# Moving weight differences, a weight product and value loads later in a fused DeltaNet and maxout FFN kernel

## Chip, cores and metric

The kernel runs on one core of one Trainium2 chip. The metric is the device time of the whole kernel in microseconds (us). The kernel before the change took 525.54 us (median of three runs, 525.25 to 526.2).

## The reference

Two blocks follow each other. The first is a DeltaNet recurrence over 768 positions, for 4 batches and 8 heads of dimension 48; the second a feed-forward block on the 3072 tokens that come out, with 384 inputs and 768 hidden units, the largest of three products each:

```python
for t in range(S):
    y[:, :, t] = q_t @ state
    v_old = state.T @ k_t                     # k_t is normalized
    state = state + beta_t * outer(k_t, v_t - v_old)
x = y.transpose(0, 2, 1, 3).reshape(B * S, H * D)
h = np.maximum(np.maximum(x @ w1, x @ w2), x @ w3)
out = h @ w_out
```

## The kernel before

**Tiling.** The positions are cut into 12 chunks of 64; a chunk is handled for all batches and heads at once, and two chunks make a group. The group's 512 tokens then go through the feed-forward block. So there are six periods, `ffn(0)` to `ffn(5)`, and the recurrence of group m+1 is worked into the period m in small portions. The text calls `ffn(0)` the first period and `ffn(1)` the second.

**A period.** `ffn(m)` is a generator. Each `yield` ends a step: in `hidden` a step multiplies one 128-wide slice f of one weight matrix with the tokens (three matmuls at L926, each of which the trace shows as two records) and takes the result out of PSUM, by a copy on ACT (L934) or ReLU (L936), or by a maximum on DVE (L940). The steps of the output multiply h with `w_out` (L958), copy on ACT and store on SP (L967). The first period has 31 steps, 0 to 30: 18 on halves of the tokens for slices 0 to 2, nine on all tokens for slices 3 to 5, four outputs. Later periods have 12 hidden and 8 half output steps.

**Less work from the second period on.** The largest of three products is also x w1 + max(0, x (w2 - w1), x (w3 - w1)), and x w1 w_out is x times one 384 x 384 matrix. So in the first period all three matrices are used; then `less_first(f)` takes w1's slice f from those of w2 and w3 (two subtractions on DVE, L883), `turn_first` transposes two slices of w1 (PE L892, ACT L898), and `both_layers(t)` makes a third of the matrix w1 w_out (PE L906, ACT L913) in w1's place. Later periods use two matrices in `hidden` and add the small matrix in their outputs.

**The recurrence.** For each group the code needs the grams of keys and queries (`gram`, PE L438, mask on DVE L422, copy on ACT L455), the inverse of triangular blocks (`solve`), and then per chunk: `join_z` (L709, copies L712 and L714), `join_u` (L723, L683), `turn_t1` (DVE L632, L634), `old_k` and `old_q` (L740, DVE L752), `new` (L768), `step` (L791, DVE L798), `to_y` (L810, DVE L812), `to_x` (L824, ACT L874). `solve` is a generator too; its pieces are pairs of DVE operations, a product (L565) and a subtraction (L569). The last three pieces write the solution to DRAM (`y_d`, L591) and read it back in another order into `ut` (L600), by SP's queue. The grams go to DRAM (`at_d`, L468) and back as `x_bl` (L515), which opens the next `solve`.

**Weights and values.** A weight comes as raw bits (`fetch`, L215, into one of five buffers `w_bits`) and is converted in the first period by `weights`: three operations on ACT (L238 to L240), and one call later a shift on DVE (L250) and an integer add on POOL (L254). `load_v` (L139) loads a chunk's values, into one of three buffers; `prep_values` scales them on POOL (L287).

**What sets the order.** The whole order is written by hand (`manual_schedule`), one queue for each engine, and each engine works in order. The loops at the end of the kernel run through the steps and issue after each step what tables and conditions say: `EARLY_LINKS` and `FIRST` name portions of the recurrence by letter and chunk or unit (z `join_z`, j `join_u`, d `turn_t1`, k, q `old_k`, `old_q`, u `new`, s `step`, y `to_y`, x `to_x`, g `gram`, t and T transposes of keys and queries, P grams of queries, S pieces of `solve`); `CONVERTED` and `FETCHED` say when weights are converted and fetched; `some(solving, n)` issues n pieces. PSUM buffers come in two rings: `ffn` with two buffers, so a hidden step needs the buffer of the step two before it, and `two` with three buffers for the recurrence and the transposes.

Of the kernel before, what the change touches and what calls it, by code (L numbers as in the profile page):

```python
# [23 lines left out]
def kernel(  # L24
# [31 lines left out]
    nc = tc.nc  # L56
# [23 lines left out]
    def ps_ffn(shape, name):  # L80
        return psum.tile(shape, FP32, name=name, tag="ffn", bufs=2)

    def ps_two(name):
        return psum.tile([128, 2, 512], FP32, name=name, tag="two", bufs=3)
# [24 lines left out]
    def rows(bb):  # L109
        return slice(C * bb, C * (bb + 1))  # L110
# [19 lines left out]
    def load_k(n, queues=one_queue):  # L130
        load(k, kpad[place(n)], n, queues)

    def load_q(n, queues=one_queue):
        load(q, qpad[n % NQ], n, queues)

    def load_v(c, queue=nc.sync):
        vts[c] = work.tile([128, 2, H, D], FP32, name="v_t", bufs=3)
        for bb in range(2):
            queue.dma_start(  # L139
                out=vts[c][rows(bb)].rearrange("p g h d -> p (g h) d"),  # L140
                in_=v[2 * bb : 2 * bb + 2, :, c * C : (c + 1) * C, :].rearrange(
                    "b h p d -> p (b h) d"
                ),
            )
# [66 lines left out]
    def fetch(queue=nc.scalar):  # L211
        if fetched[0] < len(pieces):
            _, src, (a, b) = pieces[fetched[0]]
            st = work.tile([128, 2 * 384], U32, name="w_bits", bufs=5)
            queue.dma_start(  # L215
                out=st.rearrange("p (a b) -> p a b", a=a), in_=src
            )
            staged.append(st)
            fetched[0] += 1
# [66 lines left out]
    def scale(c, nrm):  # L286
        nc.gpsimd.tensor_tensor(  # L287
            out=vts[c], in0=vts[c],
            in1=nrm[:, :, :, None].to_broadcast([128, 2, H, D]), op=ALU.mult,
        )  # L290

    def prep_values(c):

        if c in nrms:
            scale(c, nrms.pop(c))
# [214 lines left out]
    def blocks(m):  # L510
        if m == 1:
            xs[m] = in_wo(0)
        else:
            xs[m] = work.tile([128, 2, HB * BL + HB], FP32, name="x_bl", bufs=1)
        nc.sync.dma_start(  # L515
            out=in_rows(xs[m]),
            in_=at_d[m].rearrange("c f b h j i -> (c f b h) j i"),
        )
# [361 lines left out]
    def less_first(f):  # L880
        part = (slice(None), slice(None), slice(f * 128, (f + 1) * 128))
        for i in (1, 2):
            nc.vector.tensor_tensor(  # L883
                out=w_sb[i][part], in0=w_sb[i][part], in1=w_sb[0][part],
                op=ALU.subtract,
            )

    def turn_first(fs):
        p_f = ps_two("p_t")
        for i, f in enumerate(fs):  # L890
            for t in range(KT):
                nc.tensor.transpose(  # L892
                    p_f[:, i, t * 128 : (t + 1) * 128],
                    w_sb[0][:, t, f * 128 : (f + 1) * 128],
                    ident,
                )
        for i, f in enumerate(fs):
            nc.scalar.copy(  # L898
                w_sb[0][:, :, f * 128 : (f + 1) * 128],
                p_f[:, i, 0 : KT * 128].rearrange("p (t x) -> p t x", t=KT),  # L900
            )

    def both_layers(t):
        p_m = ps_ffn([128, DM], "p_m")
        for f in range(FT):
            nc.tensor.matmul(  # L906
                p_m,
                w_sb[0][:, t, f * 128 : (f + 1) * 128],
                wo_sb[:, f],
                start=(f == 0),  # L910
                stop=(f == FT - 1),
            )
        nc.scalar.copy(w_sb[0][:, t, 0:DM], p_m)  # L913
# [58 lines left out]
    def some(gen, n):  # L972
        for _ in range(n):
            if next(gen, gen) is gen:
                break

    conv = weights()
    solving = solve(0)
# [96 lines left out]
    for n in (2, 3):  # L1075
        masked(pts[n], by_par(pts[n]))
    load_q(4)
    load_v(2)
    solving = solve(1)
    some(solving, 1)  # L1080

# [7 lines left out]
    }  # L1089
    EARLY_LINKS = {  # L1090
        9: "k0 q0", 10: "t0", 11: "t1", 12: "g0", 13: "t2", 14: "g1", 15: "t3",
        16: "g2", 17: "g3", 18: "d0 d1 z0 z1", 19: "j0", 20: "j1 u0", 21: "s0",
        23: "k1 y0 q1", 24: "u1 x0", 25: "s1", 26: "y1", 28: "x1",
    }


    FIRST = {
        0: "f1 s0 S1 S1", 1: "z1 d1 S1 k1 S1 S1", 2: "j1 S1 S1 S1",
        3: "S1 q1 S1 S1", 4: "u1 T4", 5: "y1", 6: "s1 T5", 7: "x1 T6",
        8: "T7", 14: "P4", 15: "P5", 21: "P6", 22: "P7",  # L1100
    }


# [11 lines left out]
    def links(m, names):  # L1115
        for name in names.split():
            f, i = name[0], int(name[1])
            if f in RECURS and m < GROUPS:
                RECURS[f](2 * m + i)
            elif f in MADE and m + 1 < GROUPS:  # L1120
                MADE[f](2 * (m + 1) + i)
            elif f in UNIT and m + 1 < GROUPS:
                UNIT[f](4 * (m + 1) + i)
            elif f == "N" and m + 2 < GROUPS:
                load_blocks(4 * (m + 2) + i)

    def queries(names):
        for name in names.split():
            f, n = name[0], int(name[1])
            if f not in OF_KEYS:  # L1130
                links(0, name)
                continue
            OF_KEYS[f](n)
            if f == "T" and n + 3 < 11:
                load_q(n + 3)

    CONVERTED = {*range(6), *range(11, 25)}
    FETCHED = {8: 1, 12: 1, 13: 1, 14: 1, 18: 2, 19: 2, 20: 1, 21: 1}  # L1140
    for i, _ in enumerate(ffn(0)):
        if 0 < i < 7:
            fetch(nc.sync)
        for _ in range(FETCHED.get(i, 0)):
            fetch(nc.gpsimd)
        if i in (18, 25):
            some(conv, 1)
        if i == 20:
            solving = solve(2)
            some(solving, 1)  # L1150
        if i == 21:
            some(solving, 3)
        queries(FIRST.get(i, ""))
        links(1, EARLY_LINKS.get(i, ""))
        if i in CONVERTED and i != 18:
            some(conv, 1)
        if 3 < i < 14:
            some(solving, (2, 1, 2, 2, 3, 3, 3, 3, 2, 2)[i - 4])
        if i in (5, 7):
            prep_values(i // 2)  # L1160
        if i in (1, 7):
            for n in range(2):
                load_k(8 + 2 * (i > 1) + n, (nc.gpsimd, nc.gpsimd))
        if i == 0:
            load_v(3)
        if i in (0, 2):
            load_q(5 + i // 2)
        if i == 11:
            load_q(11, (nc.gpsimd, nc.gpsimd))
        if i in (10, 21):  # L1170
            load_v(4 + i // 21)
        if i == 18:
            blocks(2)
        if i == 23:
            prep_values(4)
        if i > 21:
            some(solving, (3, 2, 3, 2, 2, 5, 5, 5, 4)[i - 22])
        if i in (27, 28, 29):
            load_blocks(i - 15, nc.sync)
        if i in (15, 17, 19, 22, 25, 27):  # L1180
            less_first((15, 17, 19, 22, 25, 27).index(i))
        if 27 <= i < 30:
            turn_first((2 * (i - 27), 2 * (i - 27) + 1))


    RECURS.update(x=y_blocks, w=read_y, X=turn_y, p=prep_values)
# [2 lines left out]
    for m in range(1, GROUPS):  # L1189
        for i, _ in enumerate(ffn(m)):  # L1190
            if i == 0:
                some(solving, 3)
            if m == 1 and i in (2, 5, 8):
                both_layers(i // 3)
            if m + 2 < GROUPS:
                if i == 6:
                    blocks(m + 2)
                if i == 8:
                    solving = solve(m + 2)
            links(m + 1, LINKS.get(i, ""))  # L1200
            if i > 7:
                some(solving, 3 if i > 8 else 1)
# [29 lines left out]
```

## Time and profile before

| | |
|---|---|
| median of the runs | 525.54 us |
| the profiled execution, whole | 524.22 us |
| its span, first to last instruction | 522.5 us, granted PE clock 0.966 |
| PE, DVE, ACT, POOL busy | 495.1, 311.0, 164.4, 190.6 us |
| 40 to 120 us: PE, DVE busy | 71.25, 70.11 of 80 us |
| 120 to 522 us: PE, DVE busy | 397.77, 211.93 of 402 us |
| first step of `ffn(0)`, of `ffn(1)`, of `ffn(2)` begins | 51.0, 166.0, 250.7 us |

The profile is one execution, read by the hardware profiler. In the slices each digit is the busy share of a fortieth of the span (13 us) in tenths. In the windows, each engine has its busy time and number of instructions, then come the granted PE clock, the share of the DMA engines in use and GB/s. In the time-ordered views a line has start, duration, engine, source line, operation, tiles, shape and number of instructions; a bracket gives the idle time of the engine before it and what ended it.

### The profile page before, as it was taken

Reading aid. Unit: us, or ns where it says so; the run is one execution under the profiler, and the core shown is the slowest. Engines: PE = TensorE matmul, PEld = TensorE weight load, DVE = VectorE, ACT = ScalarE, POOL = GpSimd, SP = SyncE. Lnnn points to the kernel's source line nnn. Section 1 sums busy time; section 2 is a strip of 40 time slices with the busy share of each in tenths; the row PEclk is TensorE's granted clock in tenths of the full one; section 3 lists DMA queues with packets and bytes.
Section 4 is the critical chain, followed back from the end, with each engine's and each line's share of the span. In section 5 each row is a group of like instructions: output and inputs, shape, how many; then the busy total and the mean of one; then the engine's idle time right before and its main releaser. Section 6 shows DMA issues by size and latency. Waiting matters only on the chain.

```text
span 522.5 us, 18030 instructions
## 1 busy us (share of the span) xinstructions
PE 495.1 (95%) x7840; PEld 305.9 (59%) x7840; DVE 311.0 (60%) x695; ACT 164.4 (31%) x302; POOL 190.6 (36%) x314
## 2 busy tenths in 40 slices
PE   6667898989999999999999999999999999999996
PEld 6556686855666555665556565655655555554453
DVE  5876999998995441699652988645897221111100
ACT  5557473776513142200143200242101411011000
POOL 7515155684383844951394780502130000000000
PEclk9855899999999999999999999999999999999999
DMA  8974958476035953444585444823343202220011
GB/s 111 214 154 114 162 163 138 133 154 199 3 89 135 188 90 69 135 125 115 111 157 121 111 131 102 171 43 91 81 109 85 43 3 63 61 61 0 0 30 32
DMA packets 108671, 53.47 MB, mean 102 GB/s; under 512 B 91760, under 2 KB 102928, under 8 KB 108592
## 3 DMA queue, kind: packets, MB, share of 16 engines
q1 hardware_dynamic: 97840, 34.44, 32.3%
q0 software_dynamic: 8640, 17.49, 13.5%
q8 instruction: 62, 1.02, 0.9%
q10 hardware_dynamic: 2112, 0.39, 0.5%
q14 instruction: 17, 0.14, 0.1%
HBM read 39.17 MB, written 13.11 MB: 100 GB/s over the span
## 4 chain that ended last, share of the span: by engine, by line
PE 79%; DVE 12%; ACT 2%; DMA 2%; issue 1%; POOL 1%; SPq 1%; DVEq 0%; ACTq 0%; POOLq 0%
PE p_h L926 34%; PE p_o L958 26%; PE p_g L438 3%; DVE tmp L565 3%; PE p_m L906 2%; PE p_u L768 2%; PE p_y L810 2%; DVE wo_sb L569 2%; DMA kmore<-in_k_dram 2%; PE p_k L740 2%; PE p_j L723 2%; PE p_s L791 1%; PE p_q L740 1%; SPq L120 1%; PE p_z L709 1%
## 5 line engine op out<-in xcount | busy, mean ns | idle before, releaser
L926 PE MATMUL p_h<-xt,w_sb 128*128 128x512 f32 (+1 forms) x522 | 218.9, 564 | 2.8 <-DVE h L940 1.3
L926 PEld LDWEIGHTS p_h<-xt,w_sb 128*128 128x128 f32 x522 | 96.1, 193 | 88.2 <-issue 79.5
L958 PE MATMUL p_o<-wo_sb,h 128*128 128x384 f32 x288 | 97.8, 489 | 0.0
L940 DVE TENSOR_TENSOR h<-h,p_h 128x512 f32<-128x512 f32 (+1 forms) x48 | 29.6, 617 | 90.0 <-PE p_h L926 89.9
L958 PEld LDWEIGHTS p_o<-wo_sb,h 128*128 128x128 f32 x288 | 53.7, 190 | 35.7 <-issue 0.5
L565 DVE TENSOR_TENSOR tmp<-x_bl,y_bl 128x31 f32<-128x31 f32 (+20 forms) x139 | 51.7, 372 | 4.1
L964 ACT COPY o_sb<-p_o 128x384 f32<-128x384 f32 x24 | 11.5, 479 | 134.2 <-PE p_o L958 128.1
L569 DVE TENSOR_TENSOR y_bl<-y_bl,tmp 128x31 f32<-128x31 f32 (+20 forms) x139 | 48.5, 349 | 4.8
L936 ACT ACTIVATE h<-p_h 128x512 f32<-128x512 f32 x30 | 17.9, 597 | 87.7 <-PE p_h L926 84.8
L958 PE MATMUL p_o<-w_sb,xt 128*128 128x384 f32 x120 | 42.0, 486 | 0.0
L396 POOL DMA_DIRECT2D turned<-in_q_dram x72 | 39.1, 551 | 3.9 <-POOL turned L391 2.9
L438 PE MATMUL p_g<-kqt 48*64 48x64 f32 (+1 forms) x1216 | 27.5, 239 | 6.8 <-DVE nt_bl L263 3.8
L438 PEld LDWEIGHTS p_g<-kqt 48*64 48x64 f32 x1216 | 24.3, 139 | 14.8 <-ACT kqt L367 8.0
L958 PEld LDWEIGHTS p_o<-w_sb,xt 128*128 128x128 f32 x120 | 22.8, 190 | 15.9
L120 POOL DMA_DIRECT2D kpad<-in_k_dram x32 | 21.8, 689 | 15.8 <-PE p_s L791 14.3
L287 POOL TENSOR_TENSOR v_t<-v_t,nrm 128x768 f32<-128x768 f32 x12 | 18.2, 1518 | 24.9 <-DVE nrm L266 12.1
L254 POOL TENSOR_TENSOR w_sb<-mant,up 128x384 int32<-128x384 int32 x18 | 18.3, 1018 | 24.3 <-DVE mant L250 21.7
L798 DVE TENSOR_TENSOR st<-st,p_s 48x768 f32<-48x768 f32 (+1 forms) x18 | 17.1, 949 | 15.0 <-PE p_s L791 14.8
L422 DVE TENSOR_TENSOR pt<-p_g,mask 128x512 f32<-128x512 f32 x20 | 13.7, 688 | 15.8 <-PE p_g L438 15.8
L139 POOL DMA_DIRECT2D v_t<-in_v_dram x12 | 9.9, 827 | 35.9 <-PE p_u L768 35.9
L391 POOL MEMSET turned<- 128x96 f32 x18 | 3.3, 191 | 44.8 <-DVE kqt L412 44.8
L768 PEld LDWEIGHTS p_u<-v_t,ut 64*64 64x64 f32 x768 | 13.5, 141 | 7.8 <-issue 7.3
(153 smaller groups left out, 624.5 us busy)
## 6 DMA issues: line engine op xcount, KB each, us to landing
w_bits<-in_moe_w_dram SPq DMA_DIRECT2D x14, 384.0 KB
out_dram<-o_sb SPq DMA_DIRECT2D x48, 96.0 KB
turned<-in_q_dram POOLq DMA_DIRECT2D x72, 48.0 KB, 2.9
kpad<-in_k_dram POOLq DMA_DIRECT2D x32, 96.0 KB, 4.9
y_x<-y SPq DMA_DIRECT2D x16, 192.0 KB
qall<-y_x SPq DMA_DIRECT2D x32, 96.0 KB
ut<-y_d SPq DMA_DIRECT2D x40, 64.0 KB
v_t<-in_v_dram SPq DMA_DIRECT2D x12, 192.0 KB
```

Of the source, the lines that this page charges most:

```text
L120: queues[bb].dma_start(out=dst[rows(bb ^ g), :, 0:D], in_=src[2 * bb + g, :, c * C : (c + 1) * C, :].rearrange("h p d -> p h d"),)
L254: nc.gpsimd.tensor_tensor(out=dst.bitcast(I32), in0=mant_v.bitcast(I32), in1=up_v, op=ALU.add)
L287: nc.gpsimd.tensor_tensor(out=vts[c], in0=vts[c], in1=nrm[:, :, :, None].to_broadcast([128, 2, H, D]), op=ALU.mult,)
L396: (queue, nc.gpsimd)[i].dma_start(out=t[p0 : p0 + 32, bb, at : at + NP * 2 * D].rearrange("p (j x) -> p j x", j=NP), in_=(k, q)[i][2 * bb ...
L438: nc.tensor.matmul(p_g[rows(bb ^ (g * i)), par, c0 : c0 + C * (1 + whole)], kq[:, 0], kq if whole else kq[:, i],)
L565: nc.vector.tensor_tensor(out=t_v, in0=row.to_broadcast(t_v.shape), in1=column.to_broadcast(t_v.shape), op=ALU.mult,)
L569: nc.vector.tensor_tensor(out=rest, in0=rest, in1=t_v, op=ALU.subtract)
L768: nc.tensor.matmul(p_v[rows(bb ^ g), g, i], ut[c % NU][rows(bb), g, h], rhs[rows(bb), g, h],)
L926: nc.tensor.matmul(p_h, w_sb[i][:, t, f * 128 : (f + 1) * 128], xt[:, t, lo : lo + w], start=(t == 0), stop=(t == KT - 1),)
L936: nc.scalar.activation(out=h, in_=p_h, func=mybir.ActivationFunctionType.Relu)
L940: nc.vector.tensor_tensor(out=h, in0=h, in1=p_h, op=ALU.max)
L958: nc.tensor.matmul(p_o, stays, moves, start=(n == 0), stop=(n == len(terms) - 1))
```

## The change

Nothing is computed in another way; operations are issued at other steps or from other queues.

- `less_first`: from steps 15, 17, 19, 22, 25, 27 of the first period to its steps 29, 30 and steps 1, 3, 5, 7 of the second.
- `turn_first`: from steps 27 to 29 of the first period to steps 2, 5, 8 of the second; `both_layers`: from steps 2, 5, 8 of the second to 9, 10, 11.
- Pieces of `solve(1)`: 1, 1, 1, 1, 2, 3, 3, 3, 3, 3, 2 in steps 4 to 14 for 2, 1, 2, 2, 3, 3, 3, 3, 2, 2 in steps 4 to 13.
- The joins of the next group and nearly all that follow them in the first period come one step later (z in 19 for 18, and so on), as do the grams P6 and P7.
- A weight is converted in step 10 and none in 18; the six fetches from step 18 on go by SP's queue for POOL's.
- `load_v(2)` from before the first period to step 3, `load_v(3)` from step 0 to 8, `load_v(5)` from 21 to 22; `prep_values(2)` and `(3)` from steps 5 and 7 to 8 and 12; `load_q(5)` and `(6)` from steps 0 and 2 to 1 and 3.

```diff
     load_q(4)
-    load_v(2)
     solving = solve(1)
...
-        16: "g2", 17: "g3", 18: "d0 d1 z0 z1", 19: "j0", 20: "j1 u0", 21: "s0",
-        23: "k1 y0 q1", 24: "u1 x0", 25: "s1", 26: "y1", 28: "x1",
+        16: "g2", 17: "g3", 19: "d0 d1 z0 z1", 20: "j0", 21: "j1 u0", 22: "s0",
+        24: "k1 y0 q1", 25: "u1 x0", 26: "s1", 27: "y1", 29: "x1",
...
-        8: "T7", 14: "P4", 15: "P5", 21: "P6", 22: "P7",
+        8: "T7", 14: "P4", 15: "P5", 22: "P6", 23: "P7",
...
-    CONVERTED = {*range(6), *range(11, 25)}
+    CONVERTED = {*range(6), *range(10, 18), *range(19, 25)}
...
-            fetch(nc.gpsimd)
-        if i in (18, 25):
+            fetch(nc.gpsimd if i < 18 else nc.sync)
+        if i == 25:
             some(conv, 1)
...
-        if i in CONVERTED and i != 18:
+        if i in CONVERTED:
             some(conv, 1)
-        if 3 < i < 14:
-            some(solving, (2, 1, 2, 2, 3, 3, 3, 3, 2, 2)[i - 4])
-        if i in (5, 7):
-            prep_values(i // 2)
+        if 3 < i < 15:
+            some(solving, (1, 1, 1, 1, 2, 3, 3, 3, 3, 3, 2)[i - 4])
+        if i in (8, 12):
+            prep_values(i // 4)
...
-        if i == 0:
-            load_v(3)
-        if i in (0, 2):
+        if i in (1, 3):
             load_q(5 + i // 2)
...
-        if i in (10, 21):
-            load_v(4 + i // 21)
+        if i in (3, 8, 10, 22):
+            load_v((3, 8, 10, 22).index(i) + 2)
...
-        if i in (15, 17, 19, 22, 25, 27):
-            less_first((15, 17, 19, 22, 25, 27).index(i))
-        if 27 <= i < 30:
-            turn_first((2 * (i - 27), 2 * (i - 27) + 1))
+        if i > 28:
+            less_first(i - 29)
...
+            if m == 1 and 8 < i < 12:
+                both_layers(i - 9)
+            if m == 1 and i in (1, 3, 5, 7):
+                less_first((i + 3) // 2)
             if m == 1 and i in (2, 5, 8):
-                both_layers(i // 3)
+                turn_first((2 * (i // 3), 2 * (i // 3) + 1))
```

## The prediction

> **What bounds the kernel now.** I read the page (busy shares, slices), then ten-microsecond windows, then the time-ordered views of PE, and of DVE, POOL and SP around each gap of PE. "Step n" is a pass of the loop over ffn(0), the first period; "step B n" one over ffn(1), the second.
>
> ```profile
> PE   6667898989999999999999999999999999999996
> DVE  5876999998995441699652988645897221111100
> ```
> ```profile
> 70.00:80.00 10.00, 8.83 (x194) 7.34 (x186) 9.73 (x19) 7.27 (x14) 4.48 (x5) 1.00 0.62 165
> 80.00:90.00 10.00, 8.68 (x166) 7.50 (x166) 9.52 (x21) 2.85 (x5) 5.31 (x7) 1.00 0.91 143
> 110.00:120.00 10.00, 8.24 (x206) 4.22 (x204) 8.25 (x12) 7.74 (x15) 9.63 (x14) 1.00 0.74 203
> 160.00:170.00 10.00, 10.00 (x122) 5.98 (x122) 4.00 (x16) 2.42 (x5) 0.75 (x2) 1.00 0.50 121
> ```
>
> PE (first figure after the window's length) is full from 118 us on, and DVE (third) is full before. So time is won only where PE waits before 118 us, and lost where a wait opens later. The gaps that the change can reach are these; the bracket is PE's idle time and what ended it:
>
> ```profile
> 79.83 0.65 PE L361 MATMUL p_t<-ident,qall 128*128 128x128 f32 x4 [1.17 <-DVE st L798]
> 83.54 0.67 PE L926 MATMUL p_h<-xt,w_sb 128*128 128x256 f32 x2 [1.32 <-DVE h L940]
> ...
> 111.97 2.84 PE L926 MATMUL p_h<-xt,w_sb 128*128 128x512 f32 x6
> 116.17 0.24 PE L723 MATMUL p_j<-z,t 32*32 32x32 f32 x2 [1.36 <-ACT z L712]
> 116.78 0.74 PE L723 MATMUL p_j<-z,t 32*32 32x32 f32 x62 [0.36 <-ACT z L714]
> 117.44 1.12 PE L926 MATMUL p_h<-xt,w_sb 128*128 128x512 f32 x2
> ```
>
> The early pair is 1.17 + 1.32 = 2.5 us. The late one: from 111.97 to 117.44 are 5.47 us, and the same work elsewhere takes 2.77 (a step, 126.44 to 129.22 in the chain) + 0.68 (p_j at 120.28): 2.0 us lost. Why DVE is late at the early pair:
>
> ```profile
> 79.70 0.83 DVE L565 TENSOR_TENSOR tmp<-wo_sb 128x255 f32<-128x255 f32 x1
> 80.56 1.58 DVE L569 TENSOR_TENSOR wo_sb<-wo_sb,tmp 128x255 f32<-128x255 f32 x1
> 82.18 0.42 DVE L565 TENSOR_TENSOR tmp<-wo_sb 128x256 f32<-128x256 f32 x1
> ```
> ```profile
> 78.60 3.27 POOL L287 TENSOR_TENSOR v_t<-v_t,nrm 128x768 f32<-128x768 f32 x2
> ```
>
> Two things stand ahead of st and h in DVE's queue: pieces of the substitution (L565, L569), and the time that a POOL operation takes from them (1.58 us beside one, 0.42 alone).
>
> **What the Trainium skill says.** GPSIMD Engine Reference, section 1 Specifications: its SBUF interfaces are shared with VectorE, with contention for DVE instructions of two SBUF inputs. The rows above agree. DMA: Bandwidth & Descriptors, "Issuing engines are not separate DMA queues": another issuing engine saves only issue time; the trace gives 0.55 to 0.76 us per L215 on POOL. TensorE: Matmul & The Clock Gate, "What's actually happening": after an idle window of about 3.4 us PE falls to half clock. Here PEclk is 1.00 from 70 us on and the waits are under 1.4 us, so I count no change of clock.
>
> **The change part by part.**
>
> *Thinning.* Before step 7's end 3 pieces fewer are issued (1+1+1+1 for 2+1+2+2), and both value products (L287) move from steps 5 and 7 to 8 and 12. I laid DVE's new order out by hand with the durations of before. The st of step 6 ends near 79.0 instead of 79.8 and the maximum of step 7 near 80.2 instead of 83.3: PE reaches step 9 at 81.3, not 83.54. Gain 2.2 us. But all pieces must still be done before the joins. Up to the last piece DVE now also has one more maximum (0.33) and two more shifts L250 (0.27 each), each followed by a POOL L254 that costs it about 0.7 (1.11, 0.99 and 1.02 for rows that take 0.2 to 0.4): 2.3 us, so the solution ends near 100.9 instead of 98.75. Steps 9 to 13 with 3 pieces each push the maximum of step 13 to 98.5 or 99.1 (without, with a full collision with L287), where step 15 needs its buffer; it began at 99.55. The mask of the grams of step 14 comes near 101.3 to 102.0 and holds step 15's transposes. Step 18 thus begins between 0.3 us earlier and 0.4 later than 107.66: the early gain is given back. I take 0, bounds -0.4 and +2.0.
>
> *Joins a step later; differences gone from steps 15, 17, 19; POOL's loads on SP.* DVE loses 1.83 + 2.48 + 2.31 = 6.6 us of L883 between 103.8 and 119, POOL four L215 (2.2 us) in the stretch 114 to 117, and no weights piece stands in ACT's queue before z. z follows step 19, whose 2.77 us cover the landing of the solution (y_d issued near 101, in the trace 11 us from that to the last landing: 112; z1 comes at 113.5). The copies of z are then hidden by step 20. The 2.0 us go, and 0.26 of z (1.54 us at 110.43, 1.28 at 184.75). What is late next: in the built order the copy of step 18's h waits for a PE count reached only at z's end, so step 20 waits some 0.2. Net +2.1; bounds +0.5 (solution 1.6 us later) and +2.3. The six weight loads on SP stand behind the ut loads; their pieces were due 2 us later: 0. SP's x_bl stands behind two of them, whose buffers are free by then: 0.
>
> *Loads of values and queries.* load_v(2) and (3) leave SP's queue at 50.5 (3.9 us of issue) and stand at steps 3 and 8. No wait of PE, DVE or ACT between 50 and 76 us names them or what they push back: 0. v(2) is issued near 67 and needed at 81; v(3) is needed at step 24.
>
> *First period's end.* turn_first leaves the four outputs: three groups of 0.66 us, which return in the second period: 0. The differences of slices 0 and 1 stand after the last pieces. Before, DVE was done here, and idle to 169.94:
>
> ```profile
> 164.21 0.21 DVE L569 TENSOR_TENSOR y_bl<-y_bl,tmp 128x31 f32<-128x31 f32 x1
> 169.94 0.95 DVE L752 TENSOR_TENSOR v_t<-v_t,p_k 128x768 f32<-128x768 f32 x1 [5.52 <-PE p_k L740]
> ```
> DVE starts 2.6 us earlier and is spared three differences (3 x 1.02), so slice 0 is ready near 159.5; step B 0 begins near 161.5. 0, and 1 us at most if DVE is 3 us later. The other four pairs (1.02 each) lie in DVE's idle time of 170 to 212.
>
> *Products later.* The three p_m (3.96 each) move from steps B 2, 5, 8 to B 9, 10, 11, with 0.66 of transposes in their places. PE's sum is the same, but what waits for SP or DVE now has less cover:
>
> ```profile
> 152.44 1.17 SPq L967 DMA_DIRECT2D out_dram<-o_sb  x2
> ...
> 170.69 2.19 SPq L591 DMA_DIRECT2D y_d<-y_bl  x2
> 174.19 4.04 SPq L600 DMA_DIRECT2D ut<-y_d  x8
> ```
> SP runs without a gap from the first output (PE 151.73) to y_d; the last ut packet in the trace ends at 181.9: 30.1 us after. PE came to z1 33.6 us after it (185.3). Now: p_y 1.0, outputs and p_x 12.4, steps B 0, 1, 2 with p_k, p_q 9.9, transposes 0.7, grams 2.0, step B 3 2.8, z0 0.65: 29.45. So z1 waits 0.6 us; bounds 0 and 3. At step B 10 PE needs the maximum of B 9, which DVE reaches 7.9 us after p_s (212.6 to 220.5), behind st, y and the opening of solve(3); PE needs 1.0 + 2.7 + 4.0 = 7.7: 0.3 us, bounds 0 and 0.8.
>
> Sum: 0 + 2.1 - 0.6 - 0.3 = 1.2 us less. The profiled execution took 524.22 (span 522.5 and 1.7 around it), 1.3 below the median of 525.54; the difference applied to the median gives 524.3.
>
> **Rivals.**
> B, the early gain stays: collisions with POOL fall beside operations that read PSUM, step 15 isn't held. Then 2.0 us more: 522.3. For it: DVE's L798 took 0.94 beside L287, undisturbed. Against it: DVE has the same work, and no gap from 65 to 98 us.
> C, slower: z in the second period waits for ut. The chain SP output, blocks, y_d, ut has no slack left. Each us that the landing slips costs PE one; without that wait the sum is -1.8, so from a wait of 2.9 us on (landing 32.3 us after the first output) the kernel is slower by over 1.05. At 3.5 us: 527.2. For it: the last three of the eight ut loads took 1.0, 1.1 and 1.5 us beside values and keys, the first five 0.5 to 0.7 each. Against it: half of ut, z0's, is there at 26.1.
> D, the late wait only changes its name: the solution ends 2.2 us later and its at_d writes now stand ahead of ut on SP, so z waits in step 19 for ut what j0 waited for z: 525.5. Against it: a whole step lies between.
>
> **Chances.** A change of 0.2% (1.05 us) is about what a measurement of this kernel can tell from none. Forecast 0.45 (own range 523.3 to 525.3: 0.25 faster, 0.20 same), B 0.25 (faster), D 0.17 (same), C 0.13 (slower). Faster 0.50, same 0.37, slower 0.13. The range runs from 522.0 (B, and the 0.3 that its late wait may add) to 526.6, C's point of decision; beyond lie C's 0.13 and under 0.07 of B.
>
> **What would show it.** Right: no PE gap of over 0.5 us before L361 near 79 and L926 near 81; a gap before step 15 (ended by DVE h) or its transposes; p_j without a gap; a gap of 0.3 to 1 us in p_z of the second period, ended by ut's landing. Wrong: PE at step 18 before 106.5 (B); a PE gap before p_z at 112 (D); over 2.5 us at p_z in the second period (C); a PE gap at step B 0 ended by L883, or PEclk under 1.00 after 76 us, which nothing above counts.

## The result, and the profile after

The changed kernel takes 529.32 us (median of 6 runs, 528.11 to 529.81) against 525.54 (6 runs, 523.49 to 527.11): ratio 1.0068, 95% interval 1.0045 to 1.0092. It is slower by 3.8 us, where 524.3 was forecast. The profiled execution took 529.45, its span is 527.7, 5.2 more than before: the one profiled before lies 1.3 below its median, so the two traces differ by more than the medians.

The page's slices, and the windows (engines in the order PE, PE's weight loads, DVE, ACT, POOL):

```profile
PE   6666999798999999999999999999999999999996
DVE  5877999946978664449662888654887231111100
PEclk9856899998999999999999999999999999999999
```
```profile
70.00:80.00 10.00, 9.13 (x166) 7.52 (x165) 9.76 (x19) 7.42 (x15) 5.39 (x8) 1.00 1.13 210
80.00:90.00 10.00, 10.00 (x176) 8.85 (x175) 9.66 (x19) 4.94 (x9) 3.53 (x4) 1.00 1.11 162
110.00:120.00 10.00, 9.86 (x211) 4.99 (x210) 4.15 (x10) 6.87 (x14) 6.20 (x10) 1.00 0.64 164
120.00:130.00 10.00, 7.71 (x138) 4.08 (x139) 7.10 (x23) 7.14 (x14) 4.98 (x5) 0.83 0.72 228
160.00:170.00 10.00, 9.30 (x32) 5.35 (x31) 9.24 (x28) 1.76 (x3) 3.36 (x7) 1.00 0.66 155
```

The two places where time was to be won are won: PE is busy 1.3 us more from 80 to 90 and 1.6 more from 110 to 120. What pays for it stands in the slice and window of 120 to 130. Before, PE was busy there for 10.00 of 10 us at full clock; now for 7.71, and the clock is 0.83. The same window before:

```profile
120.00:130.00 10.00, 10.00 (x270) 6.14 (x270) 9.16 (x26) 6.44 (x13) 3.28 (x4) 1.00 0.55 168
```

PE's gaps in the changed kernel, in order of time:

```profile
79.17 0.66 PE L361 MATMUL p_t<-ident,qall 128*128 128x128 f32 x4 [0.19 <-DVE st L798]
...
92.74 1.56 PE L926 MATMUL p_h<-xt,w_sb 128*128 128x256 f32 x6 [1.01 <-DVE h L940]
100.68 1.56 PE L926 MATMUL p_h<-xt,w_sb 128*128 128x256 f32 x6 [2.42 <-DVE h L940]
103.59 0.66 PE L361 MATMUL p_t<-ident,kpad 128*128 128x128 f32 x4 [0.73 <-DVE pt L422]
126.81 4.21 PE L926 MATMUL p_h<-xt,w_sb 128*128 128x512 f32 x6 [2.29 <-DVE tmp L565]
```

The starts of like steps, before and after: step 9 at 83.54 and 81.39 (2.15 ahead), step 18 at 107.66 and 109.58 (1.9 behind), step 21 at 122.06 and 119.87 (but now j1 and u0, 1.9 us, are still to come, so the two are nearly level), B 0 at 165.99 and 168.44 (and 1.97 of transposes fewer ahead of it), the first step of the third period at 250.59 and 255.94. After that the two run alike. So the loss is made at steps 13 to 16, from step 22 to B 0, and in the second period. Step 22 is the new place:

```profile
116.44 2.81 PE L926 MATMUL p_h<-xt,w_sb 128*128 128x512 f32 x6
119.19 0.75 PE L723 MATMUL p_j<-z,t 32*32 32x32 f32 x64
119.87 2.84 PE L926 MATMUL p_h<-xt,w_sb 128*128 128x512 f32 x6
122.64 0.75 PE L723 MATMUL p_j<-z,t 32*32 32x32 f32 x64
123.32 1.20 PE L768 MATMUL p_u<-v_t,ut 64*64 64x48 f32 x64
```

The joins (L723) follow without a gap: the late wait is gone. But then PE stands from 124.52 to 126.81, and the step takes 4.21 instead of 2.84: 2.3 + 1.4 = 3.7 us.

**The bracket misleads.** It names an operation that ended nearby in time, L565, which began at 126.61. In the program as built, step 22 waits for two things: the maximum of step 20, which DVE ended at 120.70, and an integer add of weights (L254) that POOL had made before 112. Both were met four microseconds earlier. What was not there shows in the DMA queues. The first answer is for 118.06 to 124.10, the second for 124.10 to 125.20 (packets, MB, share of the 16 engines):

```profile
q1 hardware_dynamic: 587, 1.76, 82.8%
```
```profile
q1 hardware_dynamic: 118, 0.30, 70.3%
q8 instruction: 1, 0.02, 5.8%
```

Queue q8 brings instructions: by the page it has 62 packets and 1.02 MB in the whole run, so 16 KB each, one for every 126 of the 7840 matmuls. The packet that falls here started at 124.11 and landed at 125.13; PE had issued 2368 matmuls then, and issued none until 126.81. I call this theory F: PE ran out of instructions, it starved. The transfers that the packet met come from SP; the last line is x_bl's issue before the change:

```profile
111.94 0.96 SPq L215 DMA_DIRECT2D w_bits<-in_moe_w_out_dram  x2
117.96 0.33 SPq L515 DMA_DIRECT2D x_bl<-at_d  x1
118.39 2.11 SPq L215 DMA_DIRECT2D w_bits<-in_moe_w_out_dram  x4
```
```profile
115.14 0.34 SPq L515 DMA_DIRECT2D x_bl<-at_d  x1
```

SP keeps its order. x_bl waits until 117.96 for at_d to land, and four weight loads stand behind it and leave with it: 2 MB at once, the burst of what follows, and DMA is 0.99 in use from 119.5 to 124.

The rivals to F: S, PE waits after all for the opening of solve(2), which x_bl holds up in ACT's and DVE's queues; G, the loss is the thinning's give-back, that is, the early gain lost again at steps 13 to 16.

### The profile page after: what moved, and what is told of

Read it like the earlier page. It is cut to its first block, busy times and chain, and to the rows that moved or that the text cites. A ratio compares the mean times of both kernels' runs of the same rounds, so it can differ in the third digit from the quotient of the medians.

```text
span 527.7 us, 18038 instructions
## 1 busy us (share of the span) xinstructions
PE 495.3 (94%) x7840; PEld 305.5 (58%) x7840; DVE 309.3 (59%) x695; ACT 164.5 (31%) x302; POOL 187.0 (35%) x308
## 3 DMA queue, kind: packets, MB, share of 16 engines
q8 instruction: 62, 1.02, 0.8%
## 4 chain that ended last, share of the span: by engine, by line
PE 76%; DVE 13%; DMA 4%; ACT 3%; issue 2%; POOL 1%; SPq 0%; ACTq 0%; DVEq 0%
PE p_h L926 33%; PE p_o L958 25%; PE p_g L438 3%; DVE wo_sb L569 2%; PE p_u L768 2%; PE p_k L740 2%; DVE tmp L565 2%; PE p_q L740 2%; PE p_y L810 2%; PE p_s L791 1%; PE p_m L906 1%; DMA qall<-in_q_dram 1%; PE p_j L723 1%; DMA kpad<-in_k_dram 1%; PE p_z L709 1%
## 5 line engine op out<-in xcount | busy, mean ns | idle before, releaser
L964 ACT COPY o_sb<-p_o 128x384 f32<-128x384 f32 x24 | 11.5, 479 | 133.9 <-PE p_o L958 133.9
L565 DVE TENSOR_TENSOR tmp<-x_bl,y_bl 128x31 f32<-128x31 f32 (+20 forms) x139 | 50.3, 362 | 4.1
L254 POOL TENSOR_TENSOR w_sb<-mant,up 128x384 int32<-128x384 int32 x18 | 18.2, 1009 | 30.2 <-DVE mant L250 17.1
L812 DVE TENSOR_TENSOR y<-qs,p_y 128x768 f32<-128x768 f32 x11 | 10.5, 953 | 20.2 <-PE p_y L810 20.1
L752 DVE TENSOR_TENSOR v_t<-v_t,p_k 128x768 f32<-128x768 f32 x11 | 10.5, 951 | 15.9 <-PE p_k L740 15.9
```

What stands on the lines that cost most here:

```text
L254: nc.gpsimd.tensor_tensor(out=dst.bitcast(I32), in0=mant_v.bitcast(I32), in1=up_v, op=ALU.add)
L565: nc.vector.tensor_tensor(out=t_v, in0=row.to_broadcast(t_v.shape), in1=column.to_broadcast(t_v.shape), op=ALU.mult,)
```

## Experiments

Each ratio is to runs of the kernel before on the same chip (median 524.8 to 525.3), with its 95% interval. Runs named a, c and e alter the changed kernel; those named b, m and d alter the kernel before.

### Where the packet border falls

a_shift puts 120 more PE instructions at the very start:

```diff
-    busy(6, ident)
+    busy(4, ident)
+    p_w = ps_ffn([128, TOK], "p_w")[0:32, 0:32]
+    for _ in range(32):
+        nc.tensor.matmul(p_w, ident[0:32, 0:32], ident[0:32, 0:32])
```


> The changed kernel; two 128-wide warm-up products at the very start are replaced by 32 products of 32 x 32 (some 60 PE matmuls and as many weight loads more, 120 instructions, where PE waits for the first keys anyway). Nothing of the work, its order or its loads changes. Theory F: [...]the packet that starved step 22 is asked for about one step earlier, ahead of the burst of loads: the gap there goes or moves, 525.5 to 527. Theory S: same waits, 529.3 within 0.3. Theory G: 529.3.

a_shift2 puts 64 PE matmuls into p_h ahead of step 14's product:

```diff
                 p_h = ps_ffn([128, TOK], "p_h")[:, 0:w]
+                if (m, f, lo, i) == (0, 1, TOK // 2, 2):
+                    for _ in range(32):
+                        nc.tensor.matmul(
+                            p_h[0:32, 0:32], ident[0:32, 0:32], ident[0:32, 0:32]
+                        )
```


> The changed kernel with 32 products of 32 x 32 (64 PE matmuls, 0.7 us) added ahead of step 14's third product, where PE waits 2.4 us for the maximum of step 13 soon after. Nothing else moves; its own lines stand 5 lower below L918. Theory F (PE out of instructions at step 22): the packet border falls 64 matmuls earlier in the work and is asked for before the burst of loads; no gap at step 22, no half clock, 3.7 us less than the changed kernel, near 525.6. Theory S (a semaphore from the solution's opening): gap stays, 529.3 to 530. Theory G (give-back of the thinning): 529.3 to 530.

Measured: a_shift 532.14 (1.0151, 1.0091 to 1.0212), a_shift2 530.54 (1.0103, 1.0060 to 1.0146). As a time, F's expectation failed twice. In the traces the gap goes. PE in a_shift:

```profile
125.89 0.75 PE L723 MATMUL p_j<-z,t 32*32 32x32 f32 x64
126.70 0.32 PE L768 MATMUL p_u<-v_t,ut 64*64 64x48 f32 x4
127.31 1.14 PE L768 MATMUL p_u<-v_t,ut 64*64 64x48 f32 x60 [0.29 <-ACT ut L683]
128.38 2.84 PE L926 MATMUL p_h<-xt,w_sb 128*128 128x512 f32 x6
```

Step 22 follows u0 at once, at full clock; the packet started at 122.64, as the burst began (x_bl was issued at 122.17). From the start of step 21 to that of step 23 PE takes 9.68 us, in the changed kernel 12.63. But a_shift began ffn(0) 3.2 us later, and a gap of 1.31 us that no semaphore explains came at L740 (143.10), 1.40 after another packet landed: it moved. In a_shift2 the packet landed at 121.36; now u0 waits 1.68 + 0.29 us for ACT's copies of ut behind x_bl, which is S, and the half clock follows. So F is right on the gap of this trace, S is a second wait close behind it, and neither is the whole loss.

The count of matmuls supports F more firmly than these times. The gap that moved stands after 2751 matmuls in both shifted kernels (1.31 and 0.87 us), though one has 60 more in front and the other 64. The twenty traces of this case have 44 gaps of over 0.15 us that the view puts to "issue", that is, to nothing it shows. Each ends 1.2 to 1.8 us after a packet landed, and their counts (597, 723, 1105, 1232, 1358, 1485, 1738, 2751, 3384 and some later ones) lie 126 to 128, or whole multiples of that, apart. The 2368 of step 22 is one of that row.

### The loads on another queue, spread, or apart from the opening

```diff
-            fetch(nc.gpsimd if i < 18 else nc.sync)
+            fetch(nc.gpsimd)
```


> The changed kernel with one line undone: all weight loads of the steps from 18 on are issued by POOL again. Theory F (PE runs out of instructions before step 22: the 16 KB packet of its instruction stream starts only at 124.11 and lands at 125.13, when the block load and four weight loads, all on SP, have passed): POOL issues the four later and with joins between, so the packet comes through earlier; no gap of 2.3 us before step 22, no half clock after it, 3.7 us less than the changed kernel, near 525.6. Theory S (PE waits for the opening of the solution on DVE, which the block load holds up, as the trace's bracket has it: DVE tmp L565): the block load starts a little earlier, gap smaller by about 1 us, 528. Theory G (the loss is the give-back of the thinning): no change, 529.3.

529.21 (1.0069, 1.0042 to 1.0096). POOL issues four of the loads in nearly the same microseconds (117.1 to 119.3; DMA 0.97 in use from 119.5 to 124), and S appears. ACT:

```profile
124.34 0.26 ACT L261 ACTIVATE root_bl<-x_bl 128x32 f32<-128x32 f32 x1 [0.41 <-DMA x_bl<-at_d]
124.62 1.20 ACT L683 ACTIVATE ut<-p_j 32x512 f32<-32x512 f32 x2
```

u0 waits 0.92 + 0.29 for that copy. c_open moves the block that opens solve(2) in step 20 behind the joins:

```diff
-        if i == 20:
-            solving = solve(2)
-            some(solving, 1)
         queries(FIRST.get(i, ""))
         links(1, EARLY_LINKS.get(i, ""))
+        if i == 20:
+            solving = solve(2)
+            some(solving, 1)
```


> The changed kernel with one block moved: the opening of solve(2) in step 20 stands after the joins of that step instead of ahead of them, so that on ACT the copies of ut from j0 no longer queue behind root_bl, which waits for the block load. Theory S (the wait for the block load, in ACT's and DVE's queues, is what holds u0 and step 22): ut's copies come 2 us earlier; the loss at step 22 falls from 3.7 us to under 1, 526 to 527. Theory F (PE out of instructions): u0 starts no earlier than j1 ends, the gap before step 22 stays where a packet lands late, 529 within 1.

529.58 (1.0107, 1.0073 to 1.0140): the gap stays, though at 0.92 us in its trace, and so does the loss; S is not the cause of the gap. c_spread issues one load per step:

```diff
-    CONVERTED = {*range(6), *range(10, 18), *range(19, 25)}
-    FETCHED = {8: 1, 12: 1, 13: 1, 14: 1, 18: 2, 19: 2, 20: 1, 21: 1}
+    CONVERTED = {*range(6), *range(10, 18), *range(20, 26)}
+    FETCHED = {8: 1, 12: 1, 13: 1, 14: 1, 18: 1, 19: 1, 20: 1, 21: 1, 22: 1, 23: 1}
...
-        if i == 25:
+        if i == 26:
```


> The changed kernel with the last six weight loads one per step from 18 to 23 (it has 2, 2, 1, 1 from 18 to 21) and the last conversions a step later. They still stand on SP. Theory F: DMA is no longer full from 120 to 124, the 16 KB packet lands in time, no gap at step 22 and no half clock: 525.5 to 527. Theory S: the block load lands sooner too, by about 1 us: 527.5 to 528.5. If DMA load isn't the cause, 529.3.

529.93 (1.0103, 1.0077 to 1.0129). It spread nothing: SP held four of the loads behind x_bl, and they left together from 117.8 to 120.3. PE in c_open, then in c_spread:

```profile
126.72 2.81 PE L926 MATMUL p_h<-xt,w_sb 128*128 128x512 f32 x6 [0.92 <-DVE bl L541]
```
```profile
127.93 4.39 PE L926 MATMUL p_h<-xt,w_sb 128*128 128x512 f32 x6 [2.12 <-DVE y_bl L569]
```

Three runs, three names in the bracket, one fact behind them: PE resumes 1.59 and 1.46 us after its packet lands (125.13 and 126.47), as it did after 1.68 in the changed kernel.

### Each part alone

a_thin undoes the thinning (with values(3) loaded at step 5):

```diff
-        if 3 < i < 15:
-            some(solving, (1, 1, 1, 1, 2, 3, 3, 3, 3, 3, 2)[i - 4])
-        if i in (8, 12):
-            prep_values(i // 4)
+        if 3 < i < 14:
+            some(solving, (2, 1, 2, 2, 3, 3, 3, 3, 2, 2)[i - 4])
+        if i in (5, 7):
+            prep_values(i // 2)
```


> The changed kernel with the thinning undone: pieces 2,1,2,2,3,3,3,3,2,2 from step 4 on, value products back at steps 5 and 7, values(3) loaded at step 5. The early waits (1.2 and 1.3 us) come back, the waits of steps 13 to 16 (1.0, 2.4, 0.7) go; PE stands 1.9 us earlier at step 18. Theory G: the 1.9 us come through, 527.4 or less. Theory F: the time is decided by whether the instruction packet again meets the burst: about 529 if it does, about 525 if it doesn't. Theory S: the block load starts 2 us earlier against the same PE, gap at most 0.5 us, about 526.

528.85 (1.0084, 1.0060 to 1.0107). As the whole cause G is out: without the thinning the kernel is as slow as with it. Step 22 starves again (packet at 124.95, resumed at 126.48). m_join is the kernel before with the joins a step later (the two tables as in the change, left out here), their conversions, and SP's loads:

```diff
...
-    CONVERTED = {*range(6), *range(11, 25)}
+    CONVERTED = {*range(6), *range(10, 18), *range(19, 25)}
...
-            fetch(nc.gpsimd)
-        if i in (18, 25):
+            fetch(nc.gpsimd if i < 18 else nc.sync)
+        if i == 25:
...
-        if i in CONVERTED and i != 18:
+        if i in CONVERTED:
```


> The kernel before with the joins, grams P6 and P7 and the conversions of the changed kernel, and its weight loads on SP from step 18 on; thinning, value loads and the second period are as before. Theory F: step 22 starves as in the changed kernel when the packet border falls there: 2 to 4 us above what the removed wait for z (2.0) gives, 525 to 528. Theory G: no thinning, nothing given back: 523. Theory S: the block load starts 2 us earlier against the same PE: 523 to 524.

528.83 (1.0064, 1.0046 to 1.0082). This part alone has as large a loss. Its step 22:

```profile
126.32 4.51 PE L926 MATMUL p_h<-xt,w_sb 128*128 128x512 f32 x6 [2.36 <-DVE tmp L565]
```

b_late is the kernel before with the second-period moves alone:

```diff
-        if i in (15, 17, 19, 22, 25, 27):
-            less_first((15, 17, 19, 22, 25, 27).index(i))
-        if 27 <= i < 30:
-            turn_first((2 * (i - 27), 2 * (i - 27) + 1))
+        if i > 28:
+            less_first(i - 29)
...
+            if m == 1 and 8 < i < 12:
+                both_layers(i - 9)
+            if m == 1 and i in (1, 3, 5, 7):
+                less_first((i + 3) // 2)
             if m == 1 and i in (2, 5, 8):
-                both_layers(i // 3)
+                turn_first((2 * (i // 3), 2 * (i // 3) + 1))
```


> The kernel before with only the second-period moves: differences of slices 0 and 1 after the last two outputs, those of slices 2 to 5 and the transposes and products in the second period. The joins stay a step earlier. All theories: DVE has no differences at steps 15 to 19, the copies of z still wait behind the weights on ACT; second period pays 0.5 to 1.0 us (j +0.54, product +0.45 in the changed kernel). No starvation of step 22 in F or S: 525.5 within 1 us. Slower by over 2 us would put the loss on these moves.

528.71 (1.0063, 1.0044 to 1.0083). I had not expected this one: it too has as large a loss, with a step 22 that doesn't wait. By the ratios two parts of the change cost 3.4 and 3.3 us, and the whole change 3.6.

### The second period

b_diff is b_late with the products in their old places (they then work on matrices of which a part is not yet transposed, so its output differs from the reference's; the amount of work is the same):

```diff
-            if m == 1 and 8 < i < 12:
-                both_layers(i - 9)
...
                 turn_first((2 * (i // 3), 2 * (i // 3) + 1))
+                both_layers(i // 3)
```


> The kernel before with the differences and transposes later (as in the changed kernel), but the three products of the matrices left at steps B 2, 5 and 8. Against the run with the products later too, which was 3.3 us slower than the kernel before: if PE came to z of the second period before ut had landed (the trace shows 1.0 us there even in its fastest execution), the 7.9 us of products ahead of z are cover, and this kernel is as fast as before, 525. If the differences are what costs (w1 and w2 not ready for step B 0 or B 3), it stays near 528.

524.78 (1.0004, 0.9984 to 1.0025): the differences and transposes cost nothing that shows, the products all of it. b_first leaves one product at B 2:

```diff
-            if m == 1 and 8 < i < 12:
-                both_layers(i - 9)
+            if m == 1 and i in (2, 10, 11):
+                both_layers(max(0, i - 9))
```


> The kernel before with differences and transposes later, and of the three products only the first left at step B 2, the others at B 10 and B 11. It forms the first product from matrices of which only a third is transposed, so its output isn't the reference's. If the 3.5 us of the moved products are cover ahead of z (step B 3), this one product of 4.0 us gives all of it back: 525 within 0.7, as with all three early. If the products at B 10 and B 11 cost by themselves (waits for the maxima and for their copies), 527 to 528.5.

527.21 (1.0045, 1.0020 to 1.0069), in the second of the two ranges expected: z no longer waits, but PE then meets the maximum of B 9 too early and waits 1.66 us at B 10's product. Two more traces of b_late, which is 528.71 in the median:

> The kernel before with only the second-period moves, once more, for a trace of an execution nearer to its middle than the first (its fastest). If z of the second period waits for ut, the bracket at p_z near 181 grows from 1.0 us to about 4. If PE starves for instructions, there is a gap that no semaphore explains after a 16 KB packet that lands late.

> The kernel before with only the second-period moves, a third trace. If the wait of z for ut is what sets its time, that wait grows with the time: 1.0 us at 524.8, 1.7 at 527.4, about 3 at 529, 4 at 530. If the wait stays near 1.5 whatever the time, the rest of the loss lies elsewhere.

The first execution traced took 524.79 us and has one wait of 1.04 us at z1, the second (527.44) one of 1.69, the third (529.82) two, in z0 and z1:

```profile
180.55 0.90 PE L709 MATMUL p_z<-ut,at 32*32 32x32 f32 x64 [0.94 <-DMA ut<-y_d]
182.53 0.25 PE L709 MATMUL p_z<-ut,at 32*32 32x32 f32 x4 [1.08 <-DMA ut<-y_d]
182.93 0.72 PE L709 MATMUL p_z<-ut,at 32*32 32x32 f32 x60
183.58 4.46 PE L926 MATMUL p_h<-xt,w_sb 128*128 128x512 f32 x6
```

2.0 us of wait, and after it a step of 4.46 instead of 2.84, at half clock: 3.6 us. The wait grows with the time, but less than expected: about 4 was named for such a time. It isn't all that makes these executions differ. Of the 2.65 us between the first and the second, 1.3 lie ahead of the first step of `ffn(0)` (51.27 and 52.58) and 0.65 in the wait; of the 5.0 between the first and the third, 2.6 are wait and clock, and 1.5 lie after the second period. b_fill puts a product of no use in front of that z (only at i = 2, without its copy):

```diff
                 turn_first((2 * (i // 3), 2 * (i // 3) + 1))
+                both_layers(0, False) if i == 2 else None
```


> The kernel before with the second-period moves, and one product of the matrices more (12 PE matmuls, 4.0 us) at step B 2, whose result nothing uses. Against those moves alone (528.7): if PE waits there for ut anyway, as in the traces (1.0 and 1.7 us) or longer, the product fills the wait and costs 4.0 less that wait: 530 to 531 for a wait of 1 to 2.5, 529 for one of 3.5 or more. If PE's own work sets the time, 532.7.

530.53 (1.0116, 1.0088 to 1.0143). From 176.38 PE has no gap up to z:

```profile
176.38 4.14 PE L906 MATMUL p_m<-wo_sb,w_sb 128*128 128x384 f32 x12 [0.57 <-ACT w_sb L898]
180.44 2.09 PE L438 MATMUL p_g<-kqt 48*64 48x128 f32 x96
182.46 2.84 PE L926 MATMUL p_h<-xt,w_sb 128*128 128x512 f32 x6
185.24 1.35 PE L709 MATMUL p_z<-ut,at 32*32 32x32 f32 x128
```

4.1 + 0.57 = 4.7 us were added. Against b_late the median rose by 1.8 and the ratio by 0.0053, 2.8 us, so about 1.9 to 2.9 us of b_late's time at this place was standing, clock included.

### One loss or both taken away

e_early loads three of the last six weights before x_bl, all by POOL; e_open adds c_open's edit:

```diff
-    FETCHED = {8: 1, 12: 1, 13: 1, 14: 1, 18: 2, 19: 2, 20: 1, 21: 1}
+    FETCHED = {8: 1, 12: 1, 13: 1, 14: 1, 15: 1, 16: 1, 17: 1, 20: 1, 21: 1, 22: 1}
...
-            fetch(nc.gpsimd if i < 18 else nc.sync)
+            fetch(nc.gpsimd)
```


> The changed kernel with the last six weight loads on POOL, at steps 15, 16, 17, 20, 21 and 22 (it has 2, 2, 1, 1 on SP from 18 to 21). Theory F (a burst of block load and four weight loads holds up PE's instruction packet): DMA isn't full from 120 to 124, the packet lands before 123, no gap before step 22 and no half clock: 3.7 us less at o0, of which z of the second period, which then comes before ut, may take 1 to 2 back: 526 to 527.5. If DMA load isn't the cause: packet at 124 to 125 as before, 529.3.

> The run e_early with, besides, the opening of solve(2) after the joins of step 20. Theory S asks for this one too: u0 no longer waits for ut copies behind root_bl on ACT (0.9 to 1.7 us in two earlier runs): 1 us less than e_early if that wait shows there, the same if not.

e_early 529.30 (1.0084, 1.0058 to 1.0110), e_open 528.33 (1.0061, 1.0036 to 1.0086). In e_early's trace step 22 no longer starves, in e_open's for 0.38 us (DMA 0.55 and 0.70 in use from 119.5 to 124, packets down at 124.10 and 123.24), and the time stays. In e_open z waits where b_late has it:

```profile
124.72 2.81 PE L926 MATMUL p_h<-xt,w_sb 128*128 128x512 f32 x6 [0.38 <-DVE bl L266]
...
182.34 0.72 PE L709 MATMUL p_z<-ut,at 32*32 32x32 f32 x60 [1.02 <-DMA ut<-y_d]
```

e_early's trace has no wait at z. The profiled executions of these two (527.31 and 527.26) lie below their medians; where e_early's others lose 2 us more was not seen, and neither kernel was tried without the thinning. m_early is m_join with both edits, so neither a starved step 22 nor late products:

> The kernel before with the joins a step later, the early weight loads of e_early and the opening after the joins; thinning, differences, transposes and products as before. If the 2.0 us of the removed wait for z are real once nothing starves step 22: 523 to 524 against 525. If they move on to DVE (q, u1 and the last outputs wait for pieces and conversions, as one earlier run showed 2.0 us of that): 525 within 0.7.

525.47 (1.0007, 0.9985 to 1.0029), 3.4 us below m_join. The removed late wait of 2.0 us doesn't show as a gain, and its trace tells why:

```profile
117.19 0.72 PE L709 MATMUL p_z<-ut,at 32*32 32x32 f32 x60 [1.02 <-DMA ut<-y_d]
117.84 4.54 PE L926 MATMUL p_h<-xt,w_sb 128*128 128x512 f32 x6
```

z waits for ut there instead, and a stretch at half clock follows: rival D. d_best kept c_spread's loads, by POOL, with m_join's joins and c_open's edit:

> The kernel before with the joins a step later, the last weight loads one per step on POOL with conversions a step later, and solve(2)'s opening after the joins of step 20; thinning, differences, transposes and products as before. If the 2.0 us of the removed wait for z are real and were eaten at step 22 (F or S), they show here: 523 against 525. If they only move on (z of the second period is set by the chain block load, solution, ut, which starts no sooner), 525 within 0.5, or later by what the block load is later.

526.67 (1.0019, 1.0000 to 1.0038): 0.25 us of starving at step 22, no wait at z, but 1.25 us within the first output for a converted weight, which its edit put a step later. Last, b_sp is the kernel before with the loads from step 18 on SP:

> The kernel before with one line changed: the weight loads of the steps from 18 on are issued by SP. Theory F: four loads leave with the block load in one burst, the packet that began at 121.5 comes 2 us later, PE runs dry near the end of step 21: 1 to 3 us slower, 526 to 528. If the burst is harmless: 525 within 0.7, or a little less, as POOL is spared four issues.

524.81 (0.9996, 0.9982 to 1.0010). The burst is there (DMA 0.91) and does no harm: the packet had started at 120.92, landed at 121.86, and PE came to its 2368th matmul only at 126.17. None of these kernels beats the one before.

## Why the prediction was wrong, step by step

| Kernel | joins' set | products late | step 22 | z, second period | ratio |
|---|---|---|---|---|---|
| m_early | yes, burst gone | no | no wait | no wait | 1.0007 |
| b_diff | no | no | no wait | no wait | 1.0004 |
| m_join | yes | no | 2.36 and half clock | no wait | 1.0064 |
| b_late | no | yes | no wait | 1.0 to 2.0, once with half clock | 1.0063 |
| e_early | yes, burst gone | yes | no wait | no wait | 1.0084 |
| e_open | yes, burst gone | yes | 0.38 | 1.02 | 1.0061 |
| changed | yes | yes | 2.29 and half clock | no wait | 1.0068 |

(Waits in us, of one trace each, of three for b_late; the ratios are of all runs. e_early shows that a trace need not have what makes its kernel slow.)

- *Thinning, 0.* The kernel without it is as slow, so the times don't contradict the 0; the trace does, for the path was mis-sized. The early 2.2 us came, step by step as forecast; the give-back at steps 13 to 16 was larger (step 18 1.9 later, not 0.4 at most). The maximum of step 13 was due at 98.5 to 99.1 and was done at 100.62; the solution was due near 100.9 (98.75 + 2.3 is 101.05) and ended at 102.62. Just ahead of that maximum DVE met two POOL operations, an integer add of weights and a value product; beside them two rows took 1.07 and 1.43 that had taken 0.30 and 0.27 before the change:

```profile
96.88 1.07 DVE L569 TENSOR_TENSOR wo_sb<-wo_sb,tmp 128x135 f32<-128x135 f32 x1
97.98 1.43 DVE L565 TENSOR_TENSOR tmp<-wo_sb 128x112 f32<-128x112 f32 x1
99.45 0.28 DVE L569 TENSOR_TENSOR wo_sb<-wo_sb,tmp 128x112 f32<-128x112 f32 x1
...
100.21 0.41 DVE L940 TENSOR_TENSOR h<-h,p_h 128x256 f32<-128x256 f32 x1
```
```profile
96.79 1.00 POOL L254 TENSOR_TENSOR w_sb<-mant,up 128x384 int32<-128x384 int32 x1 [0.58 <-DVE mant L250]
97.76 1.53 POOL L287 TENSOR_TENSOR v_t<-v_t,nrm 128x768 f32<-128x768 f32 x1
```

- *Joins a step later, +2.1.* **The first step that failed.** The wait at L723 went as forecast, but "The six weight loads on SP stand behind the ut loads; their pieces were due 2 us later: 0" and "SP's x_bl stands behind two of them, whose buffers are free by then: 0" ask only when the weights are needed. They don't ask what else stands in that queue and where the bytes go: four loads wait behind x_bl and leave with it, and PE's next packet of instructions comes too late for step 22. Instead of +2.1 the set alone measures 3.4 us of loss (m_join); with the loads earlier on POOL and the opening behind the joins it is as fast as before (m_early). In neither does the +2.1 appear: in m_early's trace z waits for ut in place of p_j.
- *Loads of values and queries, 0.* No trace shows a wait on them; not tried apart.
- *First period's end, 0, and 1 us at most if DVE is 3 us later.* DVE was later by 4.7 (last piece at 169.1, before 164.4), and the differences came so late that B 0 waited 0.70 us. The condition was met and the price right. The bracket names ACT's copy L964, which ended at 168.30; in the program as built B 0 waits for the first difference, which ended at 168.29:

```profile
167.74 1.02 DVE L883 TENSOR_TENSOR w_sb<-w_sb 128x384 f32<-128x384 f32 x2
168.91 0.21 DVE L569 TENSOR_TENSOR y_bl<-y_bl,tmp 128x31 f32<-128x31 f32 x1
```
```profile
168.44 2.81 PE L926 MATMUL p_h<-xt,w_sb 128*128 128x512 f32 x6 [0.70 <-ACT o_sb L964]
```

- *Products later, -0.6 and -0.3.* In the changed kernel's trace the size holds: from B 0 to the third period it takes 87.50 us, before 84.60, and 1.97 of that are the transposes, so 0.9 is lost, though none of it at z (0.34 at L723, 0.37 at B 10). **In the kernel before, with the second-period moves alone, the size fails.** The places are right there: z waits for ut, and B 10 for a maximum (0.3 to 0.4 in the traces). But b_late less b_diff is 0.0059 of 525, 3.1 us. I had the wait from one reckoning against one landing; it is 1.0 to 2.0 by execution, and at 2.0 the half clock adds 1.6. That is rival C, at its place and near its price.
- *The sum.* I added the parts. They don't add: 3.4 and 3.3 make 3.6. One reason is in the traces. In the changed kernel, e_early, e_open and b_late SP issues the last load of ut 29 to 32 us after the first output begins. PE comes to the half of z that waits 34.6 us after it in the changed kernel, 32.5 in b_late: with the joins a step later y1 (L810, 1.08) stands among the outputs, and B 0 waits 0.70. That is cover for ut, so the changed kernel has less to lose at z. It isn't enough in every trace (e_open comes at 34.8 and waits 1.02), and what keeps e_early and e_open slow in their other executions stays open.
- *Signs named beforehand.* No gap near 79 and 81, none at p_j, gaps at step 15 and its transposes: seen. A gap at z of the second period: not in this trace. Of the signs against, "PEclk under 1.00 after 76 us, which nothing above counts" and a gap at B 0 both came.

What stays open is how much of the starving the burst makes. That the full DMA delays the packet fits: from 119.5 to 124 it is 0.95 to 0.99 in use in the five traces that starve for 0.9 to 2.4 us, 0.70 in e_open (0.38) and 0.58 in d_best (0.25), and 0.25 to 0.61 in five that don't starve (before, a_shift, a_shift2, e_early, m_early). But it is 0.91 in b_sp, and 0.97 in a_pool, where u0 held PE until the packet was down; and before the change it is 0.98 to 1.03 in each microsecond from 117 to 121, the packet starts as late as 121.52, and PE doesn't wait. So the order counts too. In none of the twenty traces did this packet start before PE had issued 2233 of the 2368 matmuls. In the changed order the last 128 of them are j1 and u0, which take 1.9 us, and PE is then dry; before, a step of 2.84 us stands among them, and PE comes to the place 2.3 us after the landing. m_early's packet (125.42) was no later than PE's own progress asked for, and PE came to the place at 127.59. When exactly PE asks for a packet was not seen. So the starving is shown, and the burst as its larger part likely.

## What to carry to other kernels

Before you price a load at nothing on another queue, write down what it then stands behind, what leaves with it, and who else needs the DMA in that stretch; an in-order queue turns a spread of loads into a burst. Where a gap's bracket names something that the waiting instruction doesn't wait for, look at the instruction queue, and count the matmuls issued: a gap that keeps its count when work is shifted ahead of it is no wait for data. Work that is moved off one chain's way may have been the cover of the next: ask for each moved product which landing it stood in front of, and don't expect losses along one chain to add.

## What the runs showed of the hardware

- PE's instructions come in packets of 16 KB by DMA (queue q8). In seven traces (changed kernel, c_open, c_spread, a_thin, m_join and, shorter, e_open and d_best) PE stood at step 22, after 2368 matmuls, until 1.41 to 1.71 us after the packet landed. The gap of 1.93 us "issue" at 60.05 in the kernel before fits: packet down at 58.58, resumed 1.47 later. In 15 of the 20 traces PE stands there with 1105 matmuls issued, for 0.2 to 2.0 us, until 1.2 to 1.8 us after a landing.
- A short wait can cost twice. After waits of 1.0 to 2.4 us among 32x32 and 64x64 products, the next 3.41 us were at half clock (changed kernel, m_join, c_spread, a_pool, a_shift2, b_late's third trace, m_early), 1.4 to 1.7 us more; after 0.92 (c_open), 1.02 (e_open), 1.04 and 1.69 (b_late's first two) and 2.41 (a_thin) not. The Trainium skill, TensorE: Matmul & The Clock Gate, "What's actually happening", has a free-running window of 3413 ns; the 3.41 agrees: in a trace the half-clock stretches begin a multiple of it apart, so the borders of all windows can be reckoned. a_thin's wait fell on two of them (0.84 and 1.57 us). But idle time within a window doesn't decide alone: 1.02 us were enough in m_early, and 1.76 of the wait at step 15 in the changed kernel were not. What PE does in the rest of the window may count; it wasn't tried. And the prediction's reading of that page, that waits under 1.4 us are safe, is not borne out: 1.2 us in a_pool and 1.02 in m_early were enough.
